# Padding the tile of maxima by 64 bytes: the x and softplus tiles move by 128 bytes against the weights

## The chip, the cores and the metric

The kernel runs on one core of a Trainium2 chip. The metric is the device time of one execution in microseconds (us). A comparison uses the median of several executions; beside it stands one profiled execution, whose trace gives the durations of single instructions.

## The reference

Two layers follow each other. The first is an attention over a short window with a summary of the whole sequence; the second is a feed-forward layer with a softplus between two matrix products.

```python
# q, k, v: 4 batches, 8 heads, 768 positions, 64 wide; block 32, window 16
k_sum = k.reshape(B, H, nb, 32, D).max(axis=3)          # 24 block maxima of the keys
v_sum = v.reshape(B, H, nb, 32, D).mean(axis=3)         # 24 block means of the values
scores_l = where(|i - j| < 16, q @ k.T / 8, -1e9)
scores_s = q @ k_sum.T / 8 + log(32)
a = softmax(concat(scores_l, scores_s))
x = a @ concat(v, v_sum)                                # 3072 tokens x 512
h = x @ w_in                                            # 512 x 2048
out = (max(h, 0) + log1p(exp(-|h|))) @ w_out            # 2048 x 512
```

## The kernel before, in words

**Tiling.** The 3072 tokens are cut into 12 chunks of 256, and the chunks into groups: a group is two chunks (512 tokens), and two of the groups hold one chunk (256 tokens). The hidden width 2048 is cut into 16 slices of 128, counted by `f`. For each group and each `f` the function `feed_forward` does this:

- The first product, `product` (L820): 12 matmuls into the PSUM bank `ph`. The 512 columns of x are cut into four parts `cc`. For each, three matmuls add up: high part of the weight by high part of x (`xh`), high by low part of x (`xl`), low part of the weight by `xh`. The stationary operand, which TensorE loads ahead of the matmul, is 128 columns (512 bytes of each partition) of the weight tile `w`; the moving operand, which streams through, is 512 columns (2048 bytes of each partition) of `xh` or `xl`. In the groups of 256 tokens 256 columns stream.
- ScalarE makes the softplus of `ph` twice, once rounded to `gh` (L840) and once exactly (L844); VectorE writes the difference to `gl` (L848).
- The second product, `project` (L857): 12 matmuls into the four PSUM banks `po` (6 into two in a group of 256 tokens). Here the softplus tiles are stationary, 128 of their columns at a time (`t` counts them), and a row of 512 columns of `w` streams.

So the two products use the tiles in opposite roles: in L820 the weights are loaded and x streams, in L857 the softplus tile is loaded and the weights stream. In all there are 960 + 1152 matmuls with 512 columns and 384 with 256.

**Order.** The order of all instructions is a list of numbers in the file (`SEQUENCE`), which `order.issue(SEQUENCE)` follows (L973). It interleaves the attention of the coming groups with the feed-forward of the present one. In the plain stretches TensorE does 12 matmuls of L820, then 12 of L857, and so on.

**Attention.** For each chunk and each two pairs of heads, `attention` (L573) makes the scores in `sc` (L598), adds the mask and takes the row's maximum (VectorE, L611, into `sp` and `nm`), makes the exponential with `nm` as bias (ScalarE, L619, into `sp`, its sum into `ss`), normalizes, transposes through `tb` and DRAM into `pT`, and multiplies by the values (L689, into `xo`), from which `xh` and `xl` are written (L705, L709). The tile of maxima `nm` (L580) holds 8 numbers per partition.

**Where tiles lie.** A tile has the same address in each of the 128 partitions. Tiles of a pool get their addresses one behind the other, in the order in which they are first made. `nm` comes from the pool `work`, which keeps two buffers of it. Behind it in that pool lie, in this order, `sp`, `ss`, `pT`, `vs`, `xh`, `xl`, `q`, `v`, `gh`, `gl`, `k` and `tb`. The weights and the tiles of the first chunks' attention (`kf`, `first`, `vn`, `sp0`) lie in a pool ahead of it, as do `ident`, `ones` and `added`; the tiles named `t`, `kf`, `st`, `ob` and `ks` lie in `work` ahead of `nm`.

Of the kernel before, what the change touches and what calls it, by code (L numbers as in the profile page):

```python
# [10 lines left out]
F32 = mybir.dt.float32  # L11
# [203 lines left out]
def kernel(  # L215
# [11 lines left out]
    P = 128  # L227
# [20 lines left out]
    NU = 4  # L248
    NG = 2
    WC = 2 * DM  # L250
    KiB = 1024
    T_BUFS = 2

    order = Order()
    const = ctx.enter_context(tc.tile_pool(name="const", bufs=1))
# [5 lines left out]
    def buffer(shape, dtype, name, tag=None, bufs=None, pool=work, dynamic=False):  # L261
        return Buffer(order, pool, shape, dtype, name, tag, bufs, dynamic)
# [55 lines left out]
    class Sums:  # L318
# [12 lines left out]
        def declare(self, begin):  # L331
# [3 lines left out]
            for i in range(NHP):  # L335
                kf = buffer([P, S], F32, "kf", "t", T_BUFS, dynamic=True)
                st = buffer([P, n_t, P], F32, "st", "t", T_BUFS, dynamic=True)

# [234 lines left out]
    def attention(x, i, hp, tiles, due_x, by_pe):  # L573
# [3 lines left out]
        xh, xl = x_of(x)  # L577
        cols = slice(i * CH, (i + 1) * CH)
        sc = buffer([P, 2, DM], F32, "sc", "sc", 1, psum)
        nm = buffer([P, NG * NU], F32, "nm")  # L580
        ss = buffer([P, NG * NU], F32, "ss")

        def unit(n):
# [134 lines left out]
    def weights(f):  # L718
        order.group = f"w{f}"

        for i0, i1 in [(0, 1), (1, 2)] if f < 2 else [(0, 2)]:
            n = (i1 - i0) * DM
            tag = f"w{f}_{i0}" if f < 2 else f"w{f}"
            raw = buffer([P, n, 2], U32, "raw", tag, 1, wts)
            t = buffer([P, n], U32, "t", "t", T_BUFS, dynamic=True)
            w = buffer([P, i1 - i0, 2, DM], F32R, "w", tag, 1, wts)
# [74 lines left out]
    def feed_forward(x, f0, f1):  # L801
# [74 lines left out]
        for i in range(0, n_t, 2):  # L876
            ob = buffer([P, 2, DM], F32, "ob", "t", T_BUFS, dynamic=True)

# [56 lines left out]
    for hp in range(0, NHP, NG):  # L935
        order.group = f"a0.0.{hp}"
        own = [scratch(8 + hp + g, "first") for g in range(NG)]
        places = FirstPlaces(hp, sums, own, scratch(12 + hp // NG, "sp0"))
        for i, tiles in enumerate(places.tiles):
            n = hp // NG * len(places.tiles) + i  # L940
            attention(0, i, hp, tiles, T0 - 1.5 - 4.0 * (NHP // NG * len(places.tiles) - 1 - n), True)
# [8 lines left out]
    def attend(x, sums):  # L950
        units = [(i, hp) for i in range(len(groups[x])) for hp in range(0, NHP, NG)]
        for n, (i, hp) in enumerate(units):
            c = groups[x][i]
            order.group = f"a{x}.{i}.{hp}"
            late = starts_at[x, 0] - 4.0 - APART * (len(units) - 1 - n)
            begin = late - 18.0
            if chunks[c][1] == 0 and hp == 0:
                sums = Sums(chunks[c][0])
                sums.declare(begin - 14.0)
            attention(x, i, hp, Places(c, hp, sums, pads, begin), late, False)  # L960
        return sums
# [47 lines left out]
```

## Time and profile before

| what | value |
|---|---|
| median of 3 runs | 639.71 us (637.77, 639.71, 640.17) |
| the profiled execution | 638.97 us |
| its span, first to last instruction | 637.2 us |
| granted TensorE clock | 1.000 of full speed |
| TensorE matmuls busy | 619.4 us, 97% of the span |
| VectorE, ScalarE, GpSimd busy | 279.4, 311.9, 83.4 us |
| bytes moved by DMA | 85.72 MB |

The page of the profile gives each engine's busy time and the costliest groups of instructions by line of the code. "PE" is the matmul side of TensorE, "PEld" the loading of the stationary operand, which runs beside the matmul before. The busy time of a matmul is longer than its distance to the next, because matmuls overlap in the array; what a matmul costs in a row of them is the distance from start to start. The chain of waits follows the work that ended last back to the start, and merges equal pieces; the time from one piece's start to the next is what the piece cost.

### The profile page before, as it was taken

What the parts mean: (1) busy time and instruction counts of PE and PEld (TensorE: products, weight loads), DVE (VectorE), ACT (ScalarE), POOL (GpSimd) and SP (SyncE); (2) the same over time, 40 slices, a digit from 0 to 9 for tenths busy, and PEclk for the clock granted to TensorE, in tenths of its full rate; (3) what the DMA queues carried; (4) which work ended last, traced back from release to release, by engine and by line L of the source; (5) the groups of instructions that cost most, each with busy time, mean ns of one, the idle gap of its engine ahead of it and who ended that gap; (6) DMA issues with size and microseconds to landing.
All of it is one profiled execution on the core that took longest, in us unless ns stands there. A gap on an engine that the chain in (4) does not pass through costs nothing.

```text
span 637.2 us, 11315 instructions
## 1 busy us (share of the span) xinstructions
PE 619.4 (97%) x4348; PEld 504.1 (79%) x4348; DVE 279.4 (44%) x757; ACT 311.9 (49%) x752; POOL 83.4 (13%) x74
## 2 busy tenths in 40 slices
PE   5879999999999999999999999999999999999997
PEld 4577887988888888787777878787888888888996
DVE  4999977688634643213441445432411111341111
ACT  1879988478742555216472434562522222552222
POOL 5333432524111112001000030000000000000000
PEclk9999999999999999999999999999999999999999
DMA  8799487735678751241454653443300400311100
GB/s 297 229 305 317 173 245 212 252 91 143 217 201 242 215 153 64 71 133 42 148 163 119 175 144 110 135 131 108 98 0 1 139 0 2 107 59 61 46 1 33
DMA packets 84453, 85.72 MB, mean 135 GB/s; under 512 B 24528, under 2 KB 70192, under 8 KB 84400
## 3 DMA queue, kind: packets, MB, share of 16 engines
q1 hardware_dynamic: 84400, 85.01, 43.8%
q8 instruction: 34, 0.56, 0.3%
q14 instruction: 19, 0.16, 0.1%
HBM read 64.23 MB, written 18.35 MB: 130 GB/s over the span
## 4 chain that ended last, share of the span: by engine, by line
PE 92%; DVE 0%; ACT 0%; issue 0%
PE po L857 43%; PE ph L820 42%; PE xo L689 3%; PE sc L598 3%; DVE w L791 0%; ACT w L784 0%; DVE t L758 0%; DVE xl L709 0%; ACT ob L892 0%
## 5 line engine op out<-in xcount | busy, mean ns | idle before, releaser
L820 PE MATMUL ph<-xh,w 128*128 128x512 f32 (+1 forms) x896 | 261.5, 364 | 0.2 <-ACT xh L705 0.2
L857 PE MATMUL po<-w,gh 128*128 128x512 f32 x768 | 204.7, 396 | 0.0
L820 PEld LDWEIGHTS ph<-xh,w 128*128 128x128 f32 x896 | 161.3, 188 | 31.2 <-DVE gl L848 0.6
L848 DVE TENSOR_TENSOR gl<-ph,gh 128x512 fp32r<-128x512 f32 (+1 forms) x112 | 68.1, 611 | 230.5 <-ACT ph L844 211.2
L857 PEld LDWEIGHTS po<-w,gh 128*128 128x128 f32 x768 | 142.3, 188 | 32.6 <-issue 0.6
L820 PE MATMUL ph<-xl,w 128*128 128x512 f32 (+1 forms) x448 | 162.4, 363 | 0.4 <-DVE xl L709 0.4
L840 ACT ACTIVATE gh<-ph 128x512 fp32r<-128x512 f32 (+1 forms) x112 | 60.2, 538 | 203.2 <-PE ph L820 175.3
L857 PE MATMUL po<-w,gl 128*128 128x512 f32 x384 | 115.5, 398 | 0.0
L820 PEld LDWEIGHTS ph<-xl,w 128*128 128x128 f32 x448 | 84.3, 188 | 15.5 <-DVE xl L709 0.7
L857 PEld LDWEIGHTS po<-w,gl 128*128 128x128 f32 x384 | 71.0, 188 | 17.1 <-issue 1.0
L619 ACT ACTIVATE sp<-sp,nm 128x120 f32<-128x120 f32 x192 | 73.1, 383 | 2.7 <-DVE nm L611 2.4
L844 ACT ACTIVATE ph<-ph 128x512 f32<-128x512 f32 (+1 forms) x112 | 59.4, 532 | 0.0
L780 POOL TENSOR_TENSOR t<-t,raw 128x1024 int32<-128x1024 int32 (+1 forms) x18 | 43.6, 2426 | 79.5 <-DVE t L766 25.8
L611 DVE CUSTOM_DVE_ANT_0 sp<-sc,added 128x120 f32<-128x120 f32 x192 | 40.8, 278 | 17.6 <-PE sc L598 17.3
L840 ACT ACT_TABLE_LOAD x24 | 30.8, 1283 | 35.0 <-PE ph L820 33.1
L619 ACT ACTIVATION_READ_ACCUMULATOR sp<-sp,nm 128x1 f32 x192 | 36.0, 188 | 0.0
L705 ACT CAST xh<-xo 128x512 fp32r<-128x512 f32 x24 | 14.1, 588 | 40.4 <-PE xo L689 40.4
L709 DVE TENSOR_TENSOR xl<-xo,xh 128x512 fp32r<-128x512 f32 x24 | 16.5, 688 | 39.8 <-ACT xh L705 39.8
L632 POOL TENSOR_TENSOR sp<-sp,ss 128x960 f32<-128x960 f32 x7 | 12.5, 1792 | 102.2 <-DVE ss L627 79.2
L658 DVE STREAM_TRANSPOSE tb<-sp 128x1024 f32<-128x1024 f32 x20 | 24.8, 1241 | 2.3 <-POOL sp L632 2.0
L689 PEld LDWEIGHTS xo<-pT,v 120*64 120x64 f32 x640 | 20.3, 138 | 6.9 <-issue 6.8
L619 ACT ACT_TABLE_LOAD x18 | 23.1, 1283 | 4.9 <-DVE nm L611 4.7
(64 smaller groups left out, 386.3 us busy)
## 6 DMA issues: line engine op xcount, KB each, us to landing
squares<-tb SPq DMA_DIRECT2D x20, 512.0 KB
pT<-squares SPq DMA_DIRECT2D x80, 128.0 KB
raw<-w_in_dram SPq DMA_DIRECT2D x16, 512.0 KB
raw<-w_out_dram SPq DMA_DIRECT2D x16, 512.0 KB
kf<-kT_dram SPq DMA_DIRECT2D x16, 384.0 KB
out_dram<-ob SPq DMA_DIRECT2D x11, 512.0 KB
q<-qT_dram SPq DMA_DIRECT2D x20, 256.0 KB
st<-v_hp_dram SPq DMA_DIRECT2D x12, 384.0 KB
```

What stands on the lines that cost most here:

```text
L598: nc.tensor.matmul(unit(g * NU + h * NPAIR + i)[r * QW:(r + 1) * QW, k0:k1], lhsT=q[rows, w * QW:(w + 1) * QW], rhs=k[rows], start=True, s ...
L611: nc.vector.tensor_tensor_reduce(out=sp()[:, n], in0=unit(n), in1=added()[:, kinds.index((lows[w], lows[w + 1]))], scale=-SCALE, scalar=FL ...
L619: nc.scalar.activation(sp()[:, n], sp()[:, n], AF.Exp, bias=nm()[:, n:n + 1], scale=-1.0, accum_out=ss()[:, n:n + 1],)
L658: nc.vector.transpose(out=tb().rearrange("p k (u q) -> p u k q", q=SQ), in_=tiles.sp().rearrange("p u (k q) -> p u k q", q=SQ),)
L689: nc.tensor.matmul(xo()[h * D:(h + 1) * D, g * CH + w * QW:g * CH + (w + 1) * QW], lhsT=tiles.v(g)[:, w, h * D:(h + 1) * D], rhs=queries(g ...
L709: nc.vector.tensor_sub(out=of_x(xl), in0=of_bank(), in1=of_x(xh).bitcast(F32))
L780: nc.gpsimd.tensor_tensor(a, a, word(0, I32), op=ALU.add)
L820: nc.tensor.matmul(ph()[:, :n_x], lhsT=w1()[:, i1, part, cc * P:(cc + 1) * P], rhs=a()[:, cc, :n_x], start=cc == 0 and i == 0, stop=cc == ...
L840: nc.scalar.activation(gh()[:, :n_x], ph()[:, :n_x], AF.Softplus)
L844: nc.scalar.activation(ph()[:, :n_x], ph()[:, :n_x], AF.Softplus)
L848: nc.vector.tensor_sub(out=gl()[:, :n_x], in0=ph()[:, :n_x], in1=gh()[:, :n_x].bitcast(F32),)
L857: nc.tensor.matmul(po[t](), lhsT=a()[:, t * P:(t + 1) * P], rhs=w2()[:, i2, part], start=f == f0 and i == 0, stop=f == f1 - 1 and i == 2,)
```

## The change

`nm` gets 16 more columns of 4 bytes, which nothing reads or writes.

```diff
+    NM_PAD = 16
...
-        nm = buffer([P, NG * NU], F32, "nm")
+        nm = buffer([P, NG * NU + NM_PAD], F32, "nm")
```

A buffer of `nm` so takes 96 bytes of a partition in place of 32, and with two buffers all that lies behind them in the pool is 128 bytes further. Every engine has the same instructions in the same order as before; other addresses are the only difference. The addresses in the two programs, as remainders by 2048:

| tile | before | after |
|---|---|---|
| `w` and `raw` (all 18 buffers), `t`, `kf`, `st`, `ob` | 256 | 256 |
| `xh`, `xl` (all buffers) | 128 | 256 |
| `gh`, `gl` (all buffers) | 128 | 256 |
| `q`, `v`, `k` | 128 | 256 |
| `nm`, its two buffers | 1024, 1056 | 1024, 1120 |
| `sp` | 1088 | 1216 |
| `ss`, its two buffers | 1088, 1120 | 1216, 1248 |
| `pT` | 1152 | 1280 |
| `tb` | 1920 | 0 |

Each weight tile is 4096 or 8192 bytes per partition, `xh` and `xl` 8192, `gh` and `gl` 2048, so that a row of 512 columns of them begins at these remainders too.

## The prediction

> **What bounds the kernel now.** I read the page's head first, then the waits of TensorE, then the groups of matmuls with their shapes kept apart.
>
> ```profile
> span 637.2 us, 11315 instructions
> PE 619.4 (97%) x4348; PEld 504.1 (79%) x4348; DVE 279.4 (44%) x757; ACT 311.9 (49%) x752; POOL 83.4 (13%) x74
> ```
>
> ```profile
> PE warm L931 <- POOL ident masks.py:199: 7.3, 1, 7.3
> PE xo L689 <- ACT pT L649: 3.2, 3, 1.5
> PE sc L598 <- issue: 1.8, 2, 1.2
> PE sc L598 <- DVE nm L611: 1.2, 1, 1.2
> PE ph L820 <- DVE xl L709: 0.4, 1, 0.4
> PE ph L820 <- ACT xh L705: 0.2, 1, 0.2
> ```
>
> TensorE is busy in 619.4 of 637.2 us, and its waits add up to 14.1 us, all of them with other causes than an address. Whatever the change gives or takes must therefore come as a different pace of matmuls that run one behind the other. These are the groups that make the pace:
>
> ```profile
> L820 PE MATMUL ph<-xh,w 128*128 128x512 f32 x640 | 211.2, 396 | 0.2 <-ACT xh L705 0.2
> L857 PE MATMUL po<-w,gh 128*128 128x512 f32 x768 | 204.7, 396 | 0.0
> L820 PE MATMUL ph<-xl,w 128*128 128x512 f32 x320 | 126.3, 395 | 0.4 <-DVE xl L709 0.4
> L857 PE MATMUL po<-w,gl 128*128 128x512 f32 x384 | 115.5, 398 | 0.0
> L820 PE MATMUL ph<-xh,w 128*128 128x256 f32 x256 | 50.3, 284 | 0.0
> L820 PE MATMUL ph<-xl,w 128*128 128x256 f32 x128 | 36.1, 282 | 0.0
> ```
>
> That is 640 + 768 + 320 + 384 = 2112 matmuls with 512 columns and 256 + 128 = 384 with 256, 2496 in all. The mean of one (395 to 398 ns) is not its price, since they overlap; the price is the distance between starts. For that I took the chain of waits in a stretch in which TensorE does nothing but the two products:
>
> ```profile
> 502.77 2.78 PE ph L820 x12
> 505.55 2.78 PE po L857 x12
> 508.33 2.78 PE ph L820 x12
> ...
> 530.60 2.78 PE ph L820 x12
> ```
>
> From 502.77 to 530.60 there are ten pieces of 12: 27.83 us / 120 = 231.9 ns for each matmul. The thing to see is that every piece takes the same 2.78 us. The same reading in a late group of 256 tokens:
>
> ```profile
> 592.64 1.44 PE ph L820 x12
> 594.08 1.39 PE po L857 x6
> 595.47 1.43 PE ph L820 x12
> ```
>
> A matmul with 256 columns costs 1.44 / 12 = 120 ns, one with 512 costs 1.39 / 6 = 232 ns. So the sum that the change can act on is 2112 x 0.232 + 384 x 0.120 = 490.0 + 46.1 = 536.1 us, 84% of the span.
>
> **The change part by part.** It removes and adds no instruction, and moves none on any engine or queue; the 16 columns are never touched. All that differs is where tiles lie. There are three places where that could show.
>
> *First, the pace of the two products.* While one matmul streams, the stationary operand of the next is loaded:
>
> ```profile
> L820 PEld LDWEIGHTS ph<-xh,w 128*128 128x128 f32 x896 | 161.3, 188 | 31.2 <-DVE gl L848 0.6 <-ACT xh L705 0.6 <-issue 0.5
> ```
>
> The load takes 188 ns of the 232, so two reads of the same memory run side by side, and the question is whether their relative place matters. The kernel before has tried nearly everything already. Call d the address of the loaded operand less that of the streaming one, by remainder of 2048. In L820 x streams from 128 and the weights are loaded from 256 + 512 cc: d is 128, 640, 1152, 1664. In L857 the weights stream from 256 and the softplus tile is loaded from 128 + 512 t: d is 1920, 384, 896, 1408, thus 128 to the other side. The pieces above are 2.78 us for the one and for the other. Also x streams from 128 and the weights from 256, so a stream's own place has been tried at both values, and so has a load's.
>
> After the change d is 0, 512, 1024 or 1536. Those were there too, at the seams where one product follows the other: the last matmul of L820 streams x from 128 while the first softplus slice is loaded from 128, and the last of L857 streams weights from 256 while the next weights are loaded from 256. The second of these has exactly the addresses of after. A timeline of two seams:
>
> ```profile
> 303.70 0.63 PE L857 MATMUL po<-w,gh 128*128 128x512 f32 x2
> 304.17 0.39 PE L857 MATMUL po<-w,gl 128*128 128x512 f32 x1
> 304.40 0.40 PE L820 MATMUL ph<-xh,w 128*128 128x512 f32 x1
> 304.63 0.39 PE L820 MATMUL ph<-xl,w 128*128 128x512 f32 x1
> ...
> 306.73 0.40 PE L820 MATMUL ph<-xl,w 128*128 128x512 f32 x1
> 306.96 0.39 PE L820 MATMUL ph<-xh,w 128*128 128x512 f32 x1
> 307.19 0.63 PE L857 MATMUL po<-w,gh 128*128 128x512 f32 x2
> ```
>
> From 304.17 to 304.40 (the seam into L820) is 0.23 us, from 306.96 to 307.19 (the seam out of it) 0.23; inside the products 304.40 to 304.63 is 0.23, 306.73 to 306.96 is 0.23, and the two from 303.70 to 304.17 are 0.235 each. I took the start times of all such undisturbed distances between 512-column matmuls. The first such seam of the trace and the last stand in these rows (the last is from the second matmul of its first row):
>
> ```profile
> 57.50 0.39 PE L820 MATMUL ph<-xh,w 128*128 128x512 f32 x1
> 57.73 0.63 PE L857 MATMUL po<-w,gh 128*128 128x512 f32 x2
> ...
> 628.74 0.62 PE L857 MATMUL po<-w,gl 128*128 128x512 f32 x2
> 629.20 0.28 PE L820 MATMUL ph<-xh,w 128*128 128x256 f32 x1
> ```
>
> There are 115 seams, with a mean of 231.0 ns; the other 1929 distances have 232.7. In the quiet stretch of the chain above the sign is the other way: its 15 seams (499.6 to 538.8 us) have a mean of 232.5 against 231.9. So the equal place is worth between -1.7 and +0.6 ns for a matmul, and nothing says that it is either: a seam differs from other distances in its PSUM bank as well. If this held for all 2496, the ends would be -4.2 and +1.5 us. I take 0, because the two nearest measurements disagree in sign.
>
> One rule speaks against any effect. The Trainium skill, page "TensorE: Matmul & The Clock Gate", section "Step-by-step: what each phase is for", gives TensorE two independent read ports and says that loading the next stationary operand takes no read bandwidth from the running matmul. By it the term is exactly 0. The trace agrees as far as the place goes (2.78 us with either sign of d).
>
> *Second, VectorE and ScalarE on moved tiles.* The instructions that read or write `nm`, `ss`, `pT`, `gh`, `gl`, `xh` and `xl` may run at another speed. No row shows one of them at two addresses that differ in this way. TensorE's waits bound it: of all waits above, those for `pT` (3.2) and `nm` (1.2) could shrink, 4.4 us at most, and they fall in the first 50 us, where `sp0`, `kf` and `first` stay where they are. Behind that TensorE never waits for them, since 97% of the span is its own work; the cover is the interleaving of `SEQUENCE`. I take 0, and for the range half a microsecond to either side, about a tenth of 4.4.
>
> *Third, DMA into `q`, `v`, `k` and `pT`.* Loads for the attention end well ahead of their use; all that TensorE's loading side waits for them is in these rows:
>
> ```profile
> PEld sc L598 <- DMA v<-vs: 0.4, 1, 0.4
> PEld vt L404 <- DMA first<-v_hp_dram: 0.3, 1, 0.3
> PEld xo L689 <- DMA first<-v_hp_dram: 0.2, 1, 0.2
> ```
>
> Only the first belongs to a tile that moves. The bounds are -0.4 and, if such a wait became twice as long, +0.4; I take 0.
>
> **The sum.** The profiled execution has 638.97 us, its span 637.2 and 1.8 around it. With 0 + 0 + 0 it stays 638.97. The bounds of the terms are -4.2 - 0.5 - 0.4 = -5.1 and +1.5 + 0.5 + 0.4 = +2.4. That execution lies 0.74 us under the median of the runs, 639.71, and inside their spread (637.77 to 640.17). A median of the changed kernel's runs is drawn from the same spread; I take 639.4, between the two.
>
> **The rivals.** *Faster: the two reads collide now, and the equal place ends it.* For it speaks that a matmul does cost more than its columns. By the rows above 256 further columns cost 232 - 120 = 112 ns, so 512 cost 224, and 8 ns of each matmul belong to no column. If these 8 ns were the collision, and it went everywhere, 2496 x 8 ns = 20.0 us would go: 619.0 us. Against it: the seams have the equal place, and keep 231.0 to 232.5 where 224 would be due. I give it 5 in 100, mostly for an effect that needs many equal places in a row. The skill's price would make this rival larger: the same page, section "Wait — 56ns, not 53.3ns?", has 215.7 ns from start to start at 512 columns (measured there in bf16). By that figure 2112 x (231.9 - 215.7) = 34.2 us could go, and the time would be an estimated 604.8 us. The trace shows 231.9 for this kernel's data type.
>
> *Slower: the equal place makes them collide.* When both reads start at the same remainder (cc = 0 and t = 0, a quarter of the matmuls), the load would hold up the stream as long as they share their 512 bytes. The stream passes 512 of its 2048 bytes in 232 / 4 = 58 ns, so 624 x 58 ns = 36.2 us would come on top: 675.2 us. It decides from 3.2 us / 624 = 5.1 ns a matmul. Against it: in the 115 seams such a pair stands, and 58 ns more in them would read 0.29 where the rows have 0.23. I give it 3 in 100, for the same reason as above.
>
> *In between:* a pace shifted by about 1.3 ns or more on all 2496, which is 3.2 us and is seen at one end only of the first term. I give 3 in 100 to faster and 1 to slower.
>
> **How the numbers follow.** About 0.5%, 3.2 us, is what a measurement of this kernel can tell from no change. My forecast, no change, has 88 in 100 and lies at 639.4 us. The rivals above have 5 and 3, the small shifts 3 and 1: faster 0.08, same 0.88, slower 0.04. The range leaves out the two large rivals. Its low end is the lowest run less half of the first term's gain, 637.77 - 2.1 = 635.7, say 636.0; its high end is the highest run with the first term's loss, 640.17 + 1.5 = 641.7, say 641.5.
>
> **What would show it.** Right: pieces of 12 matmuls in the stretch from 500 to 540 us again at 2.78 us in both products, pieces with 256 columns at 1.43 to 1.44, loads at 188 ns, TensorE busy for 619 us. The first term is wrong if those pieces read under 2.77 or over 2.80 (0.02 us in 12 is 1.7 ns a matmul). The second is wrong if the span changes while the pieces don't, and the waits for `pT` and `nm` do; the third if TensorE's loading side waits for DMA by more than a microsecond. The rival on the faster side would show pieces of 2.69, the one on the slower side pieces of 2.78 + 3 x 0.058 = 2.95.

## The result, and the profile after

| | before | after |
|---|---|---|
| median | 639.39 us (637.77 to 640.17, 4 runs) | 628.93 us (627.36 to 630.34, 4 runs) |
| ratio | | 0.9839, 95% interval 0.9803 to 0.9875 |
| profiled execution, its span | 638.97, 637.2 us | 630.34, 628.5 us |

The change makes the kernel 1.6% faster, 10.5 us. A second measurement (after2, below, with 9 runs of before beside 4 of the changed kernel) has 0.9818, interval 0.9794 to 0.9842. The forecast, no change, was wrong.

The page of the changed kernel, its head, and the matmul groups with their shapes apart. Lines of the code have moved by 3, so L823 and L860 are the two products.

```profile
span 628.5 us, 11315 instructions
PE 611.5 (97%) x4348; PEld 505.5 (80%) x4348; DVE 277.5 (44%) x757; ACT 311.7 (50%) x752; POOL 83.2 (13%) x74
```

```profile
L823 PE MATMUL ph<-xh,w 128*128 128x512 f32 x640 | 207.3, 391 | 0.0
L860 PE MATMUL po<-w,gh 128*128 128x512 f32 x768 | 201.1, 392 | 0.0
L823 PE MATMUL ph<-xl,w 128*128 128x512 f32 x320 | 124.6, 390 | 0.0
L860 PE MATMUL po<-w,gl 128*128 128x512 f32 x384 | 113.7, 393 | 0.0
L823 PE MATMUL ph<-xh,w 128*128 128x256 f32 x256 | 50.4, 284 | 0.0
L823 PE MATMUL ph<-xl,w 128*128 128x256 f32 x128 | 36.2, 283 | 0.0
```

Each group with 512 columns has lost 4 to 5 ns of its mean (396 to 391 in the largest, 398 to 393 in the last); the two with 256 columns have lost nothing. The chain of waits in the quiet stretch and in the late group of 256 tokens says what a matmul costs now:

```profile
501.54 2.72 PE ph L823 x12
504.26 2.72 PE po L860 x12
...
528.74 2.72 PE ph L823 x12
```

```profile
586.91 1.43 PE ph L823 x12
588.34 1.39 PE po L860 x6
```

From 501.54 to 528.74 ten pieces of 12 take 27.20 us, 226.7 ns for a matmul where it was 231.9. The granted clock is 1.00 in this stretch in both traces, so it isn't the clock. The pieces with 256 columns were 1.43 to 1.44 us and are 1.43. And not all matmuls with 512 columns became faster: in the groups of 256 tokens they come in runs of six behind 12 matmuls with 256 columns, and such a run takes 1.39 us here, as in the rows of before that the prediction shows. The two groups have 2 x 16 x 6 = 192 of these. So the gain of 5.2 ns belongs to 2112 - 192 = 1920 matmuls: 10.0 us, nearly what the medians differ by (10.5).

The span of this profiled execution has lost 8.7 us only, because of a term that has nothing to do with the change: in its first 50 us the granted clock was 0.90 of full speed, where that of before was 1.00. The row of before, then that of after; the clock is the third number from the end:

```profile
0.00:50.00 50.00, 36.24 (x521) 28.62 (x521) 39.44 (x113) 31.66 (x92) 18.37 (x34) 1.00 0.88 281
0.00:50.00 50.00, 36.60 (x510) 28.30 (x511) 36.25 (x111) 29.67 (x90) 18.16 (x34) 0.90 0.81 256
```

In x512 and all224 (below), where the clock was 1.00 there, the first product begins at 46.43 and 45.97 us of the span, in this execution at 49.60. The four runs agree with it: two with a mean clock of 0.992 have spans of 628.4 and 628.5 us, two with 0.999 and 1.000 have 625.9 and 625.6. Against these last the span of before is 11.3 to 11.6 us longer.

The other two terms are where the prediction had them. TensorE's waits are:

```profile
PE warm L934 <- POOL ident masks.py:199: 7.1, 1, 7.1
PE xo L692 <- ACT pT L652: 2.7, 1, 2.7
PE sc L601 <- issue: 2.3, 2, 1.7
PE sc L601 <- DVE nm L614: 1.2, 1, 1.2
```

13.3 us against 14.1, and its loading side waits 0.4 us for the DMA into `v`, as before.

### The profile page after: what moved, and what is told of

Its sections match the earlier page's. It is cut to its first block, busy times and chain, and to the rows that moved or that the text cites. A ratio compares the mean times of both kernels' runs of the same rounds, so it can differ in the third digit from the quotient of the medians.

```text
span 628.5 us, 11315 instructions
## 1 busy us (share of the span) xinstructions
PE 611.5 (97%) x4348; PEld 505.5 (80%) x4348; DVE 277.5 (44%) x757; ACT 311.7 (50%) x752; POOL 83.2 (13%) x74
## 4 chain that ended last, share of the span: by engine, by line
PE 95%; DMA 1%; issue 1%; POOL 1%; SPq 1%; ACT 0%; DVE 0%; POOLq 0%; DVEq 0%
PE po L860 42%; PE ph L823 42%; PE sc L601 4%; PE xo L692 4%; DMA first<-v_hp_dram 1%; PE vt L407 1%; PE warm L934 1%; POOL added L296 0%; SPq L555 0%; PE pt L648 0%; DVE sp L614 0%; ACT sp L622 0%; SPq L738 0%; SPq L741 0%; ACT vn L420 0%
## 5 line engine op out<-in xcount | busy, mean ns | idle before, releaser
L823 PE MATMUL ph<-xh,w 128*128 128x512 f32 (+1 forms) x896 | 257.6, 360 | 0.0
L860 PE MATMUL po<-w,gh 128*128 128x512 f32 x768 | 201.1, 392 | 0.0
L823 PEld LDWEIGHTS ph<-xh,w 128*128 128x128 f32 x896 | 161.7, 189 | 27.2 <-issue 0.5
L860 PEld LDWEIGHTS po<-w,gh 128*128 128x128 f32 x768 | 142.1, 188 | 29.5 <-issue 0.5
L823 PE MATMUL ph<-xl,w 128*128 128x512 f32 (+1 forms) x448 | 160.8, 359 | 0.0
L860 PE MATMUL po<-w,gl 128*128 128x512 f32 x384 | 113.7, 393 | 0.0
L823 PEld LDWEIGHTS ph<-xl,w 128*128 128x128 f32 x448 | 84.5, 189 | 13.1
L860 PEld LDWEIGHTS po<-w,gl 128*128 128x128 f32 x384 | 71.0, 188 | 15.5 <-issue 1.0
L708 ACT CAST xh<-xo 128x512 fp32r<-128x512 f32 x24 | 14.1, 590 | 39.2 <-PE xo L692 39.2
```

The source lines that it names most:

```text
L823: nc.tensor.matmul(ph()[:, :n_x], lhsT=w1()[:, i1, part, cc * P:(cc + 1) * P], rhs=a()[:, cc, :n_x], start=cc == 0 and i == 0, stop=cc == ...
L860: nc.tensor.matmul(po[t](), lhsT=a()[:, t * P:(t + 1) * P], rhs=w2()[:, i2, part], start=f == f0 and i == 0, stop=f == f1 - 1 and i == 2,)
```

## The experiments

From here on the *distance* of a pair is the address of the loaded operand less that of the streaming one, by remainder of 256 bytes; why 256 is what the first experiments show. By that count before has 128 in both products (in the first the loaded operand is 128 bytes ahead, in the second 128 behind, and by remainder of 256 that is the same), and after has 0 in both. The table gives the runs that move all of x, all softplus tiles or everything; the two columns of pieces are the chain's pieces of 12 matmuls with 512 columns between 400 and 540 us. A single piece that differs from the others is left out: 2.75 in the first product of the four runs with 0 in both, 2.72 in that of x_only, 2.80 in that of gh_only.

| run | w; x; gh begin at (by 2048) | distance, first and second product | pieces, first and second | us |
|---|---|---|---|---|
| before | 256; 128; 128 | 128, 128 | 2.78 to 2.80, 2.78 to 2.80 | 639.39 |
| after | 256; 256; 256 | 0, 0 | 2.72, 2.72 | 628.93 |
| all384 | 384; 384; 384 | 0, 0 | 2.72, 2.72 | 629.33 |
| x512 | 256; 512; 512 | 0, 0 | 2.72, 2.72 | 628.45 |
| all224 | 224; 224; 224 | 0, 0 | 2.72, 2.72 | 627.97 |
| x_only | 256; 256; 128 | 0, 128 | 2.76, 2.80 | 634.59 |
| gh_only | 256; 128; 256 | 128, 0 | 2.79, 2.73 | 635.20 |
| x192 | 256; 192; 192 | 64, 192 | 2.80, 2.76 to 2.80 | 636.01 |
| x448 | 256; 448; 448 | 64, 192 | 2.80, 2.76 to 2.79 | 637.00 |
| x320 | 256; 320; 320 | 192, 64 | 2.76 to 2.79, 2.80 | 637.00 |
| x288 | 256; 288; 288 | 224, 32 | 2.80, 2.80 | 639.06 |
| x160 | 256; 160; 160 | 96, 160 | 2.79 to 2.81, 2.79 to 2.81 | 639.61 |

Runs of before that stood beside the others on the same chip had 638.51 (the first four), 638.59 (x192, x320, x288, all224), 639.20 (x160) and 642.34 us (x448). Where a time here is from a single run it tells little by itself; the pieces tell more.

**Relative place or absolute alignment: all384 and x512.** Against after, one moves everything by 128 bytes, the other x and the softplus tiles by 256.

```diff
 all384, against after
-    ones = Buffer(order, const, [P, 2 * NB + LINE // 4], F32, "ones")
+    ones = Buffer(order, const, [P, 2 * NB + LINE // 4 + 32], F32, "ones")
 x512, against after
-        nm = buffer([P, NG * NU + NM_PAD], F32, "nm")
+        nm = buffer([P, NG * NU + 48], F32, "nm")
```

> The changed kernel with 128 more bytes ahead of the weights, so that weights, x and softplus tiles all begin at 384 within 2048: equal places, but no multiples of 256. Theory R (what counts is the place of the loaded operand relative to the streaming one): the pieces of 12 matmuls stay at 2.72 us, the time at 0.984 of before. Theory A (each operand must begin at a multiple of 256 bytes; before, one of the two stood at 128 in either product): now both operands are off, pieces of 2.78 us or more, time at 1.00 of before or above.

> The tile of maxima padded by 48 numbers in place of 16: x and softplus tiles begin at 512, the weights at 256. Every operand is at a multiple of 256, the loaded one 256 bytes away from the streaming one, by remainder of 512. Theory R with a period of 512 or 2048 bytes: pieces of 2.78 us, time 1.00 of before. Theory A, or theory R with a period of 256: pieces of 2.72 us, 0.984 of before.

all384 has 0.985 of before (0.9814 to 0.9887), x512 0.9837 (0.9792 to 0.9881). The pieces of all384, then those of x512:

```profile
505.78 2.72 PE ph L820 x12
508.50 2.72 PE po L857 x12
```

```profile
507.10 2.72 PE po L857 x12
509.82 2.72 PE ph L820 x12
```

Both are fast. So theory A falls (in all384 none of these operands lies at a multiple of 256), and so does theory R with a period of 512 or 2048 bytes (in x512 the two places are 256 apart). What is left is the relative place with a period of 256 bytes or a part of it. A part is not enough: 128 is slow in before, so the period doesn't divide 128.

**Halves of the change: x_only and gh_only.**

```diff
 x_only, against after: q padded by 1920 bytes (the lines that use it without the padding are left out here)
-            q = buffer([P, NG, CH], F32, "q", bufs=1)
+            q = buffer([P, NG * CH + 480], F32, "q", bufs=1)
 gh_only, against before: nm as it was, q padded by 128 bytes (the same lines left out)
-            q = buffer([P, NG, CH], F32, "q", bufs=1)
+            q = buffer([P, NG * CH + 32], F32, "q", bufs=1)
```

> Half of the change: xh and xl at 256, the softplus tiles gh and gl back at 128 (480 numbers of padding behind q). Theories R and A both expect pieces of 2.72 us in the first product and 2.78 in the second, some 5.5 us off the time. If the pace is not set product by product but by what stands in a run of both, the pieces are the same in both products.

> The other half: gh and gl at 256, xh and xl at 128 (32 numbers of padding behind q, none in the tile of maxima). Theories R and A both expect 2.78 us in the first product and 2.72 in the second, some 5.5 us off. If the tile of maxima's own padding made the gain, nothing is gained here.

634.59 and 635.20 us against 638.51: 3.9 and 3.3 us less, where 5.5 were expected. The chain of x_only, then of gh_only:

```profile
504.39 2.76 PE ph L823 x12
507.15 2.80 PE po L860 x12
509.94 2.76 PE ph L823 x12
```

```profile
505.04 2.79 PE ph L823 x12
507.83 2.73 PE po L860 x12
510.57 2.79 PE ph L823 x12
```

The product whose distance is 0 is faster than the other, so each half does its own part; and gh_only gains without any padding in `nm`, so the padding of that tile is not what helps. But the equal product isn't at 2.72, and this is the most telling result of the study. Here are the mean distances between starts, in ns, counted from the seam at which the product begins (the first number is the seam itself), over all undisturbed pieces of 12 in the trace (48 of a first product, 28 of a second). The pair at the seam is an equal one in all but gh_only:

```
x_only, first product   233.0 231.8 227.0 228.6 230.1 227.9 229.2 228.6 227.1 226.9 226.7 226.6
gh_only, second product 229.9 231.8 232.1 230.8 226.4 227.1 227.3 226.7 227.2 227.0 226.5 226.8
before, second product  230.5 233.2 230.0 235.3 229.0 235.0 230.6 238.4 230.2 235.2 230.0 234.3
after, second product   226.6 226.7 226.7 226.6 226.7 226.7 226.6 226.7 226.7 226.6 226.7 226.6
```

An equal pair behind a run of unequal ones doesn't have the fast pace yet; it comes four to eight matmuls later. A seam in before is one equal pair between two runs of unequal ones. The runs of six in the groups of 256 tokens fit this: in after all their pairs are equal, and their distances, from the first start on, are 233.9, 235.1, 228.9, 232.1, 230.9 and 227.0 ns (means of 14 undisturbed runs). They end about when the fast pace begins.

**Other distances: x192, x320, x288, x160, x448.** Edits: `nm` padded by 8, 24, 16 and 40 numbers in x192, x320, x288 and x448, none in x160; x288 and x160 have 32 bytes more behind `pT`.

```diff
 x160 and x288: pT padded by 32 bytes (read and written without the padding)
-        pT = buffer([P, NG * NU * P], F32, "pT", bufs=1)
+        pT = buffer([P, NG * NU * P + 8], F32, "pT", bufs=1)
```

> The tile of maxima padded by 8 numbers: x and softplus tiles at 192, weights at 256, thus 64 bytes apart. Theory E (the places must be equal by remainder of 256, anything else costs the whole): pieces of 2.78 us, time as before. Theory G (the cost grows with the distance from a multiple of 256, largest at 128): pieces near 2.75 us, about 5 us off the time. Theory H (only half a period, 128 bytes, is bad): 2.72 us, about 10 us off.

> Padded by 24 numbers: x and softplus tiles at 320, 64 bytes to the other side of the weights. In the first product x now begins after the weights and in the second the softplus tile after them, the reverse of x192. E: 2.78 us in both products; G: 2.75 in both; H: 2.72 in both. If the sign of the distance counts, the two products change roles between this run and x192.

> The changed kernel with 32 more bytes ahead of x and the softplus tiles: 288 against the weights' 256. E: 2.78 us; G: about 2.735; H: 2.72. If 32 bytes cost more than 64 do, what counts is also a grid of 64 bytes.

> The kernel before with 32 more bytes ahead of x and the softplus tiles: these at 160, the weights at 256. The loaded operand stands 96 bytes behind the stream in the first product and 96 ahead in the second. If all unequal places cost about the same: 2.79 us in both products. If the cost falls towards the loaded operand 64 bytes ahead of the stream, as x192 and x320 suggest (230 ns there, 233 at 64 behind): under 2.78 in the second product and about 2.79 in the first.

> The tile of maxima padded by 40 numbers: x and softplus tiles at 448, weights at 256. By remainder of 256 this is x192's place in every group, by remainder of 512 it is not. Period 256: as x192, 2.80 us in the first product and 2.76 to 2.80 in the second, in the late group 1.39 for 12 matmuls with 256 columns and 1.37 for 6 with 512. Period 512 or more: other values, in the late group 1.41 to 1.42 and 1.39 as small48 had with these places.

Rows of x192, then of x320:

```profile
506.58 2.80 PE ph L820 x12
...
514.98 2.77 PE po L857 x12
```

```profile
506.66 2.76 PE ph L820 x12
509.42 2.80 PE po L857 x12
```

The sign counts, and it goes with the distance and not with the product: at 64 the means over the whole trace are 233.2 ns (first product of x192) and 233.3 (second of x320), at 192 they are 230.1 (second of x192) and 230.4 (first of x320). At 32, 96, 160 and 224 they are 233.2 to 234.0, at 128 in before 232.7 and 232.8, at 0 in after 227.1 and 227.9. The 230 isn't a pace that has yet to settle: in x192 the last four of twelve distances in the second product still have 228.2 to 231.2. Theory G falls, since 32 bytes cost as much as 128; H falls too. E holds but for 192, where half is paid.

x448 tells the period. By remainder of 256 it has x192's places, by remainder of 512 not. Its late group, then that of x192:

```profile
601.23 1.37 PE po L857 x6
602.60 1.39 PE ph L820 x12
```

```profile
600.27 1.37 PE po L857 x6
601.64 1.39 PE ph L820 x12
```

The same, and over the whole trace 233.3 and 230.1 ns against 233.2 and 230.1. The period is 256 bytes.

**A place off the 64-byte grid: all224.** `LINE = 0` in place of 32.

> The changed kernel without the 32 bytes of padding behind the tile of ones: weights, x and softplus tiles all begin at 224, still at equal places, but no longer at a multiple of 64 bytes. If only the relative place counts: 2.72 us in both products, 10 us off the time. If the operands must also begin at a multiple of 64 bytes: pieces over 2.72.

627.97 us, 2.72 in both products but for one piece of 2.75, as in after: of the places tried, only the relative one counts.

**Single pairs out of place: xl_off, xh_off, gl_off.** In each, one tile is made 256 bytes larger and used from byte 128 on.

```diff
 xl_off (xh_off the same with xh; gl_off with gl and bufs=3), against after
             x_bufs[x] = [buffer([P, NCC, CT], F32R, name, bufs=2) for name in ("xh", "xl")]
+            moved = x_bufs[x][1]
+            name = ("xh", "xl")[1]
+            def further(name=name):
+                flat = work.tile([P, NCC * CT + 64], F32R, name=name, tag=name, bufs=2)
+                return flat[:, 32:32 + NCC * CT].rearrange("p (c n) -> p c n", c=NCC)
+            moved.make = further
```

> The changed kernel with the data of xl 128 bytes further: in the first product every third matmul (xh, xl, xh for each part of x) streams from 128 bytes beside the loaded weights by remainder of 256, the other two from the same place. Theory S (the cost is a sum over pairs, 5.2 ns for an unequal one): 12 x 226.7 + 4 x 5.2 ns = 2.74 us in the first product, 2.72 in the second. Theory T (the pace belongs to a run of pairs that are all equal, and a few matmuls pass until it holds): the first product about as slow as with all unequal, 2.78 us; the second 2.72 to 2.74.

> The same with xh in place of xl: two of three matmuls of the first product out of place. Theory S: 12 x 226.7 + 8 x 5.2 ns = 2.76 us. Theory T: 2.78 us or more, no better than xl_off.

> The changed kernel with the data of gl 128 bytes further: in the second product the last four loads of twelve, one behind the other, are out of place, the eight of gh are not. Theory S: 2.74 us in the second product, 2.72 in the first. Theory T: the eight keep 226.7 ns once they have settled, the four lose it at once, and the first product, which follows, needs some matmuls to settle: over 2.74 in the second and over 2.72 in the first.

Rows of xl_off, of xh_off, of gl_off:

```profile
505.89 2.75 PE ph L827 x12
508.63 2.72 PE po L864 x12
```

```profile
507.25 2.75 PE ph L827 x12
510.00 2.76 PE po L864 x12
```

```profile
505.69 2.76 PE po L861 x12
508.45 2.72 PE ph L824 x12
```

In xl_off the distances between starts in the first product go, behind the seam, 227.0, 233.9, 226.2, 226.8, 234.0, 226.1 and so on (means of 48 pieces): an unequal pair costs its 7 ns on the spot, and its equal neighbours keep 226.1 to 227.2. Theory T falls there, and S is right but for its price (7 for 5.2 ns, 2.75 for 2.74). In xh_off, where two of three pairs are unequal, the first product takes no longer than in xl_off (2.75, below S's 2.76), but the second, all of whose pairs behind the seam are equal, has 2.76 in place of 2.72 and reaches 226.6 only nine matmuls behind the seam. In gl_off the second product has 2.75 to 2.77, over S's 2.74. But where it begins with the eight loads of `gh`, these have 226.6 to 226.7 ns from the start, and the four of `gl` 232.4, 241.0, 232.6 and 230.6 (means of 14 pieces): again about 7 ns on the spot for an unequal pair. And the first product behind it is at 2.72 and at its pace two matmuls behind the seam, as S has it. The single times are 628.83, 630.64 and 632.17 us beside 642.34 of before. So neither theory holds alone. Call the pace that a run of matmuls has settled into its rhythm. A few unequal pairs in an equal rhythm are paid one by one; behind a stretch with mostly unequal pairs the rhythm has to settle first.

**What is the fixed part: half_load.**

```diff
 half_load, against after (the new first line is broken in two here)
-  po[t](), lhsT=a()[:, t * P:(t + 1) * P], rhs=w2()[:, i2, part],
+  po[t]()[:P if i == 0 or f == f1 - 1 else P // 2],
+  lhsT=a()[:, t * P:t * P + (P if i == 0 or f == f1 - 1 else P // 2)],
+  rhs=w2()[:, i2, part],
```

> The changed kernel, in whose second product the matmuls with the low parts (the second and the third of each token tile) load 64 columns in place of 128, except in the last slice of the hidden width; it leaves out these parts for half of the tokens. The stream of 512 columns is as long as before. Theory L (at equal places a matmul costs its columns and 32 cycles of 2.4 GHz more because the load's 512 bytes are read beside the stream, a cycle for each 16 bytes): 16 cycles for a half load, so that 12 matmuls take (4 x 544 + 8 x 528) / 2400 = 2.67 us in the second product, and 2.72 in the first. Theory F (the 32 cycles belong to each matmul, whatever it loads): 2.72 in both.

The row of the shorter loads of `gh`, then two pieces:

```profile
L857 PEld LDWEIGHTS po<-w,gh 128*64 128x64 f32 x354 | 47.6, 134 | 14.3
```

```profile
500.12 2.76 PE po L857 x12
502.88 2.72 PE ph L820 x12
```

632.20 us, against 639.20 of before and 627.91 of the changed kernel on that chip. The second product became slower, 2.76 for 2.72, though its loads are shorter (a load of 64 columns has a mean of 134 ns, of 128 columns 188). Both theories fall. Putting shorter loads between the others disturbs the rhythm too. The matmuls behind these loads also write half as many partitions, and the run doesn't tell the one from the other.

**A version with the best place for each shape: after2 and small48.**

```diff
 small48, against after; likewise for gh and gl where they are written and loaded
+    SMALL = 48
...
-        cols = slice(i * CH, (i + 1) * CH)
+        o = 0 if len(groups[x]) > 1 else SMALL
+        cols = slice(o + i * CH, o + (i + 1) * CH)
-     rhs=a()[:, cc, :n_x],
+     rhs=a()[:, cc, o:o + n_x],
```

> The changed kernel once more, beside the next one on the same chip: 0.984 of before, pieces of 2.72 us, in the late group of 256 tokens 1.43 us for 12 matmuls of the first product and 1.39 for 6 of the second.

> The changed kernel, in whose two groups of 256 tokens x and the softplus tiles are written and read from column 48 on, 192 bytes further: there the loaded operand of the first product stands 64 bytes behind the stream (by remainder of 256), in the second 64 bytes ahead of it, as in x192. If the place by remainder of 256 sets the pace, whatever tile it is and however the place came about: 1.39 us for 12 matmuls with 256 columns and 1.37 for 6 with 512, as x192 has them, 2.72 for the rest, and about 2 x 16 x 0.06 = 1.9 us off the changed kernel's time. If x192's short pieces had another cause, the small groups stay at 1.43 and 1.39.

after2 has 627.91 us, small48 628.13 (ratio 0.9816, 0.9792 to 0.9841): no difference between them. The late group of small48:

```profile
600.54 1.39 PE po L860 x6
601.93 1.41 PE ph L823 x12
```

In this group it has the places of x448, which by remainder of 256 are those of x192, and not their pace: its pairs with 256 columns stay at 117 to 119 ns, while in x192 and x448 they go from 118 through 122 to 113 within each run of twelve. So the places of the two operands don't settle the pace at 256 columns alone. What stood before the group differs (equal pairs in small48, unequal ones in x192), and the places of other tiles differ too; which of them makes it is not shown.

## Why the prediction was wrong

**What bounds the kernel** was right: the gain is the pace of the two products, and the stretch and the pieces named to watch (2.78 us) are where it shows: 2.72, under the 2.77 from which the first term was to count as wrong.

**The first term is the step that failed**, in two places.

"The kernel before has tried nearly everything already." It had tried one place, eight times over. The differences 128, 640, 1152, 1664 and 1920, 384, 896, 1408 are all 128 by remainder of 256, and so are the two signs. I had put them in order by the 2048 of the change's description, and took equal pieces in both products for proof that the place doesn't matter; they show it only for places that are a multiple of 256 bytes apart. x512 and x448 show the period.

The seams were the only pairs at another place, and I read each as if it stood alone: "nothing says that it is either". x_only and gh_only show what they were: an equal pair behind a run of unequal ones keeps the run's pace for four to eight matmuls. So 115 seams (21 of which lead to a matmul with 256 columns) said nothing about 2112 equal pairs, and the bounds of -1.7 and +0.6 ns taken from them, -4.2 and +1.5 us, weren't bounds. The value was -5.2 ns on 1920, and little or nothing on the 192 with 512 columns in runs of six and on the 384 with 256 columns. The two disagreeing means (231.0 and 232.5 against 232.7 and 231.9) should have warned that a pair's price was not its own.

**The rival on the faster side**, with 5 in 100, had the right sign and the right reason: an effect that needs equal places in a row is what the runs show, though not every one in the row must be equal (xl_off). That the two reads collide, as it has it, is not shown. Its size was wrong. It took 8 ns of every matmul, 20.0 us, from the part that belongs to no column; the matmuls with 256 columns, which would have that part too, lost nothing. The difference for 256 further columns was 2.78 / 12 - 1.44 / 12 = 112 ns, and is 2.72 / 12 - 1.43 / 12 = 107.5. So the excess wasn't where I looked for it.

**The rule of two read ports.** The Trainium skill, page "TensorE: Matmul & The Clock Gate", section "Step-by-step: what each phase is for", has the load take no read bandwidth from the running matmul. What I drew from it, that the place can't matter, the trace contradicts: with the same instructions the matmul's pace changes by 5.2 of 231.9 ns with the place of the loaded operand against the stream's. The 215.7 ns that the same page gives in the section "Wait — 56ns, not 53.3ns?" at 512 columns (in bf16) isn't reached by a settled run at any place here; the best was 226.7.

**The second and third terms**, 0 and 0, were right: TensorE's waits are 13.3 us against 14.1, and its loading side waits 0.4 us for `v`, as before.

**The rival on the slower side** had the sign of the effect turned round. It also counted 624 matmuls, a quarter, where 672 begin both reads at the same remainder: in the groups of 256 tokens the second product has two token tiles, so half of its loads do.

**What stays open** is what in the chip makes the period of 256 bytes, the 13.3 ns that an equal pair still costs beyond 0.4167 ns for each of its 512 columns (the difference of 226.7 and 120.0 ns, the distances of after at 512 and 256 columns, over 256 columns), why a rhythm takes matmuls to settle, and what sets the pace at 256 columns. That load and stream are the two parties is shown by the halves and by the sign at 64 and 192: the effect goes with their distance, whichever of the two tiles is loaded. That they meet at one memory was only argued, and half_load speaks against the simplest form of it.

## What to carry to other kernels

Where matmuls run one behind the other, let the loaded and the streaming operand begin at the same address by remainder of 256 bytes: here every other place that was tried cost 1 to 3% of the pace at 512 columns. A small tile ahead of the big ones in a pool can spoil it, and 64 bytes of padding in it can mend it; look at the addresses after each edit that changes a tile's size. And before a trace is read as an experiment that was already made, ask whether its cases differ in the quantity that counts, and whether one instruction among others has a price of its own.

## What the runs showed of the hardware that was not expected

- The pace of TensorE's matmuls depends on the two operands' relative place with a period of 256 bytes: over the whole trace 227.1 to 227.9 ns at 0 (226.7 once settled), 230.1 to 230.4 at 192, 232.5 to 232.8 at 128, 233.2 to 234.0 at 32, 64, 96, 160 and 224. With 256 columns an equal place isn't the best: pieces of 12 took 1.43 us at 0 and 1.39 at 64.
- The pace has a memory: behind a run of unequal places it took equal pairs up to nine matmuls to reach 226.7 ns, and runs of six with 512 columns behind matmuls with 256 gained nothing from equal places (1.39 us before and after).
- Loads of 64 columns among loads of 128, with matmuls that write half the partitions, made a product slower (2.76 for 2.72 us in 12).
- The granted clock of the first 50 us differed between executions (0.90 and 1.00), and spans of the same kernel differed by some 2.7 us with the mean clock (0.992 and 0.999 to 1.000).
